# Attention backward with column tiles: dQ one group of four units later, a fourth buffer for the transposed dS, one for the turned dK and dV

## The chip, the cores and the metric

The kernel runs on one core of a Trainium2 chip. Its engines each have an instruction queue of their own: TensorE (PE, its weight loads as PEld), VectorE (DVE), ScalarE (ACT), GpSimd (POOL) and SyncE (SP), which here issues DMAs; 16 DMA engines move the data. The metric is the device time of one execution in microseconds (us), lower is better.

## The reference

A transformer block with adaptive layer norm (2048 tokens, width 512, 32 heads of 16, an MLP of width 1792 with squared ReLU), its output and its gradients with respect to all inputs but one. In bfloat16; the part that the change touches is the gradient of the attention.

```python
def _A_ref(x, wqkv, wo):                       # D = 512, H = 32, Dh = 16
    q, k, v = heads_of(x @ wqkv)
    p = softmax(einsum('bhqd,bhkd->bhqk', q, k) * Dh ** -0.5)
    o = einsum('bhqk,bhkd->bhqd', p, v)
    return merged(o) @ wo
...
h = layernorm(x) * (1 + ca) + sa
x = x + ga * _A_ref(h, A_wqkv, A_wo)
h = layernorm(x) * (1 + cb) + sb
x = x + gb * mlp(h)
...
_out, _vjp = jax.vjp(_f, A_x, A_wqkv, A_wo, B_w1, B_b1, B_w2, B_b2, c, w_mod)
return (_out, *_vjp(grad_out))
```

## The kernel before

The program runs in stages, one after the other: modulation and layer norm, q, k, v and the attention forward, the MLP forward and backward, then the attention backward (`attn_bwd`, L1075), and last the gradients of the qkv weights, of x and of the modulation (`phase6`). The change lies in `attn_bwd` alone, which runs from 1640.82 to 3639.30 us of the profiled span.

Heads are taken in pairs: a group `g` of four heads is loaded at once (`load_group`: the transposed q and dO, and k, q and dO by tokens), and `jp` takes its two pairs. For a pair, the 2048 keys are cut into four columns of 512 (`c`), and for each column 16 blocks of 128 queries (`ib`) follow. One column and one block is a unit, for both heads `a` of the pair. A unit does this:

- TensorE: the scores `st` (L1184) and dP, named `dp` (L1190), 128 x 512 for each head, into PSUM.
- ScalarE: `pu`, the exponential of the scores (L1194). VectorE: `ds` = `dp` times `pu` (L1195), in bfloat16, into a tile `dsg` that holds the four units of a group (`G = 4`).
- TensorE, one group later: dK and dV (`kv`, L1127), with `ds` and `pu` as moving operands, summed over the queries in `acckv` and, at the end of a column, copied out by VectorE as `kvT` (L1130), a tile of 128 x 2048 for a pair. When a pair is done, `turn` (L1136) transposes `kvT` on TensorE and ScalarE copies it to `dk_t` and `dv_t`.
- dQ needs `ds` transposed. After its four units a group issues one DMA transpose from SP (L1204), `dsg` to `dsT`, 32 blocks of 128 x 128. `dq` (L1149) takes `dsT` as weights, eight products a unit, and sums dQ of the whole pair in one PSUM bank, `accq`. The first `dq` of a pair clears the bank (L1145), the last copies it out (L1155), both on VectorE.

What orders TensorE is the program text: the stage is under `manual_schedule` for TensorE. On the other engines, a scheduler places the instructions by their dependences and the order of the text. Two lists carry work over: `pend` holds the units whose dK, dV is to come; `kv_group` runs four of them behind the second unit of the next group. `pendq` holds the units whose dQ is to come. A group's four entries are added behind its transpose (L1206), and each unit takes one off the front as long as more than `G` are there (L1197): so a group's dQ runs two groups later, one entry a unit, behind that unit's scores and dP.

Buffers come from pools, and a tile waits until the buffer that it takes over is no longer read: `ds` has three (L1090), `dsT` three (L1091), `kvT` two (L1092), `pu` nine. The loads for the next four heads (L1111 to L1118) and the next pair's masked keys and values (L458) are issued by POOL, in its queue, as soon as their buffers are free.

Of the kernel before, what the change touches and what calls it, by code (L numbers as in the profile page):

```python
# [33 lines left out]
class K:  # L34
# [1040 lines left out]
    def attn_bwd(self):  # L1075
# [7 lines left out]
        tc, nc = self.tc, self.nc  # L1083
        S, D, H, NQ, ST, SC = self.S, self.D, self.H, self.NQ, self.ST, self.SC
        G = 4
        W = 4 * DH
        with ExitStack() as es:
            qp = es.enter_context(tc.tile_pool(name="p5q", bufs=2))
            pup = es.enter_context(tc.tile_pool(name="p5pu", bufs=9))
            dsp = es.enter_context(tc.tile_pool(name="p5ds", bufs=3))  # L1090
            dtp = es.enter_context(tc.tile_pool(name="p5dt", bufs=3))  # L1091
            kvp = es.enter_context(tc.tile_pool(name="p5kv", bufs=2))  # L1092
            stp = es.enter_context(tc.tile_pool(name="p5st", bufs=2, space=PSUM))
            dpp = es.enter_context(tc.tile_pool(name="p5dp", bufs=2, space=PSUM))
            accp = es.enter_context(tc.tile_pool(name="p5acc", bufs=1, space=PSUM))
# [10 lines left out]
            pend, pendq = [], []  # L1106

            def load_group(g):
                T = {}
                for n, src in fm.items():  # L1110
                    t = qp.tile([P, S], BF16, name=f"{n}q")  # L1111
                    nc.gpsimd.dma_start(t[:], src[g])
                    T[n] = t
                for n, src in tm.items():
                    t = qp.tile([P, ST, W], BF16, name=f"{n}g")
                    with nc.allow_non_contiguous_dma(reason="128B runs"):
                        nc.gpsimd.dma_start(t[:], src.rearrange("(st p) d -> p st d", p=P)[:, :, g * W:(g + 1) * W])
                    T[n] = t  # L1118
                return T
# [12 lines left out]
            def turn(g, jp, kvT):  # L1132
                h0 = 4 * g + 2 * jp
                tp = dpp.tile([P, ST, P], BF16, name="dp")
                for st in range(ST):
                    nc.tensor.transpose(tp[:, st, :], kvT[:, st * P:(st + 1) * P], self.ident[:])  # L1136
                v = tp[:].rearrange("p s (t a e) -> p t s a e", t=2, a=2)
                for t, dst in enumerate((self.dk_t, self.dv_t)):
                    d = dst[:, :, h0 * DH:(h0 + 2) * DH].rearrange("p s (a d) -> p s a d", a=2)
                    nc.scalar.copy(d, v[:, t, :, :, 0:DH])  # L1140

            def dq(u):
                (T, g, jp, c, ib, i, dsT) = u
                if c == 0 and ib == 0:
                    nc.vector.memset(accq[:], 0.0)  # L1145
                for a in range(2):
                    col = (2 * jp + a) * DH
                    for sub in range(4):
                        nc.tensor.matmul(accq[:, ib, a, :], lhsT=dsT[:, (i * 2 + a) * 4 + sub, :],  # L1149
                                         rhs=T["K"][:, 4 * c + sub, col:col + DH], start=False, stop=False,  # L1150
                                         skip_group_check=True)
                if c == SC - 1 and ib == ST - 1:
                    h0 = 4 * g + 2 * jp
                    d = self.dq_t[:, :, h0 * DH:(h0 + 2) * DH].rearrange("p s (a d) -> p s a d", a=2)
                    nc.vector.tensor_scalar(d, accq[:], self.scale, None, ALU.mult)  # L1155

            def kv_group():
                for u in pend[:G]:
                    kv(u)
                (T, g, jp, c, ib, kvT, pu, ds) = pend[G - 1]  # L1160
                del pend[:G]
                return (g, jp, kvT) if c == SC - 1 and ib == ST - 1 else None
# [5 lines left out]
            with tc.manual_schedule(engines={mybir.EngineType.PE}):  # L1168
                for g in range(NQ):
                    Tn = load_group(g + 1) if g + 1 < NQ else None  # L1170
                    for jp in range(2):
                        if 2 * g + jp + 1 < 2 * NQ:
                            self.load_masked(masked, msrc, (2 * g + jp + 1) // 2, 1 - jp, eng=nc.gpsimd)
                        kvT = kvp.tile([P, S], BF16, name="kvT")
                        for c in range(SC):
                            c0 = 512 * c
                            for ib0 in range(0, ST, G):
                                dsg = dsp.tile([P, G, 2, 512], BF16, name="ds")
                                for i in range(G):
                                    ib = ib0 + i  # L1180
                                    q = slice(ib * P, (ib + 1) * P)
                                    sts = [stp.tile([P, 512], F32, name="st") for a in range(2)]
                                    for a in range(2):
                                        nc.tensor.matmul(sts[a][:], lhsT=T["QT"][:, q], rhs=masked["KT"][2 * jp + a][:, c0:c0 + 512],  # L1184
                                                         start=True, stop=True)
                                    if turnq and i == 3:
                                        turn(*turnq.pop(0))
                                    dp = dpp.tile([P, 2, 512], F32, name="dp")
                                    for a in range(2):
                                        nc.tensor.matmul(dp[:, a, :], lhsT=T["dOT"][:, q], rhs=masked["VT"][2 * jp + a][:, c0:c0 + 512],  # L1190
                                                         start=True, stop=True)
                                    pu = pup.tile([P, 2, 512], BF16, name="pu")
                                    for a in range(2):
                                        nc.scalar.activation(pu[:, a, :], sts[a][:], ACT.Exp, scale=self.scale)  # L1194
                                    nc.vector.tensor_tensor(dsg[:, i], dp[:], pu[:], ALU.mult)  # L1195
                                    pend.append((T, g, jp, c, ib, kvT, pu, dsg[:, i]))
                                    if len(pendq) > G:  # L1197
                                        dq(pendq.pop(0))
                                    if i == 1 and len(pend) >= G + 2:
                                        r = kv_group()  # L1200
                                        if r:
                                            turnq.append(r)
                                dsT = dtp.tile([P, 8 * G, P], BF16, name="dsT")
                                nc.sync.dma_start_transpose(dsT[:], dsg[:].rearrange("p i a k -> p (i a k)"))  # L1204
                                for i in range(G):
                                    pendq.append((T, g, jp, c, ib0 + i, i, dsT))  # L1206
                    T = Tn
                turn(*kv_group())
                while pendq:
                    dq(pendq.pop(0))  # L1210
# [264 lines left out]
```

## Time and profile before

| | us |
|---|---|
| median of 2 runs (lowest, highest) | 3818.99 (3810.42, 3827.56) |
| the profiled execution | 3816.07 |
| its span, first to last instruction | 3814.2 |
| attention backward in it | 1998.5 (1640.82 to 3639.30) |

The page cuts the span into 40 slices of 95.4 us. Each digit is the share in tenths for which the engine was busy in that slice; PEclk is TensorE's granted clock, DMA the mean share of the 16 DMA engines.

```profile
PE   5999988888767777878788787788787887788877
DVE  6222210000043653566567556566665776667755
ACT  3999999999832443345556555455554655556633
PEclk8999999999978988989889888899898999899988
DMA  3111100000134655467978878888778888788862
```

The attention forward fills slices 2 to 10: ScalarE is at 9, the DMA engines are nearly idle. The attention backward begins in the eighteenth slice and ends in the thirty-ninth: TensorE at 7 and 8, ScalarE and VectorE at 5 to 7, the DMA engines at 7 and 8, and a clock that is granted to 8 or 9 tenths.

### The profile page before, as it was taken

What the parts mean: (1) busy time and instruction counts of PE and PEld (TensorE: products, weight loads), DVE (VectorE), ACT (ScalarE), POOL (GpSimd) and SP (SyncE); (2) the same over time, 40 slices, a digit from 0 to 9 for tenths busy, and PEclk for the clock granted to TensorE, in tenths of its full rate; (3) what the DMA queues carried; (4) which work ended last, traced back from release to release, by engine and by line L of the source; (5) the groups of instructions that cost most, each with busy time, mean ns of one, the idle gap of its engine ahead of it and who ended that gap; (6) DMA issues with size and microseconds to landing.
All of it is one profiled execution on the core that took longest, in us unless ns stands there. A gap on an engine that the chain in (4) does not pass through costs nothing. (4 is left out here: it accounts for less than half of the span.)

```text
span 3814.2 us, 75626 instructions
## 1 busy us (share of the span) xinstructions
PE 3094.9 (81%) x31556; PEld 1460.3 (38%) x31556; DVE 1894.1 (50%) x2761; ACT 2354.2 (62%) x3577; POOL 371.1 (10%) x583
## 2 busy tenths in 40 slices
PE   5999988888767777878788787788787887788877
PEld 2555533333333434633333333333333333334333
DVE  6222210000043653566567556566665776667755
ACT  3999999999832443345556555455554655556633
POOL 3111100000010233010000100100001001000000
PEclk8999999999978988989889888899898999899988
DMA  3111100000134655467978878888778888788862
GB/s 127 49 49 50 50 20 6 12 11 5 38 138 146 209 147 188 131 138 145 154 140 149 147 132 136 146 142 155 148 139 142 152 149 156 137 138 155 158 192 71
DMA packets 1178339, 447.82 MB, mean 117 GB/s; under 512 B 1089162, under 2 KB 1145612, under 8 KB 1177996
## 3 DMA queue, kind: packets, MB, share of 16 engines
q1 hardware_dynamic: 1140188, 353.70, 47.2%
q0 software_dynamic: 29184, 79.59, 7.1%
q10 hardware_dynamic: 8624, 9.70, 0.8%
q8 instruction: 247, 4.05, 0.4%
q14 instruction: 96, 0.79, 0.1%
HBM read 106.83 MB, written 67.64 MB: 46 GB/s over the span
## 5 line engine op out<-in xcount | busy, mean ns | idle before, releaser
L1194 ACT ACTIVATE pu<-st 128x512 bf16<-128x512 f32 x2048 | 1105.6, 594 | 859.5 <-PE st L1184 857.9
L1195 DVE TENSOR_TENSOR ds<-dp,pu 128x1024 bf16<-128x1024 f32 x1024 | 1226.6, 1222 | 680.8 <-ACT pu L1194 413.8
L412 ACT ACTIVATE pu<-st 128x1024 bf16<-128x1024 f32 x1024 | 940.1, 1376 | 4.7 <-PE accbank L418 4.7
L1184 PE MATMUL st<-KTm,QTq 128*128 128x512 bf16 x2048 | 700.1, 400 | 39.8 <-DMA dOTq<-dOTq_d 7.4
L1149 PE MATMUL accq<-Kg,dsT 128*128 128x16 bf16 x8192 | 362.3, 171 | 366.8 <-DMA dsT<-ds 326.6
L1190 PE MATMUL dp<-VTm,dOTq 128*128 128x512 bf16 x2048 | 648.4, 400 | 0.3
L409 PE MATMUL st<-QTm,KTq 128*128 128x512 bf16 x2048 | 607.0, 377 | 6.5 <-ACT pu L412 1.5
L1149 PEld LDWEIGHTS <-dsT 128*128 128x128 bf16 x8192 | 351.0, 98 | 676.1 <-DMA dsT<-ds 419.9
L418 PEld LDWEIGHTS <-pu 128*128 128x128 bf16 x8192 | 291.2, 96 | 458.7 <-ACT pu L412 408.2
L418 PE MATMUL accbank<-Vaug,pu 128*128 128x17 bf16 x8192 | 353.5, 172 | 67.6 <-DVE accbank L405 7.4
L1190 PEld LDWEIGHTS <-dOTq 128*128 128x128 bf16 x2048 | 206.8, 101 | 353.6 <-issue 172.8
L1127 PE MATMUL acckv<-ds,Qg 128*16 128x512 bf16 x2048 | 321.5, 444 | 0.6 <-DVE ds L1195 0.6
L1127 PE MATMUL acckv<-pu,dOg 128*16 128x512 bf16 x2048 | 321.5, 444 | 0.0
L427 DVE RECIPROCAL rl<-accbank 128x4 f32<-128x4 f32 x128 | 23.0, 180 | 526.0 <-PE accbank L418 525.6
L458 POOL DMA_DIRECT2D KTm<-KTq_d x120 | 59.8, 503 | 1504.7 <-PE st L1184 1502.7
L1184 PEld LDWEIGHTS <-QTq 128*128 128x128 bf16 x2048 | 123.8, 97 | 147.3 <-issue 146.4
L288 DVE TENSOR_SCALAR ev_fm<-pps,bcol 128x512 bf16<-128x512 f32 x92 | 69.1, 751 | 195.0 <-PE pps L281 194.0
L409 PEld LDWEIGHTS <-KTq 128*128 128x128 bf16 x2048 | 129.7, 96 | 35.0 <-issue 20.6
L281 PE MATMUL pps<-xhat1T,wpad 128*128 128x512 bf16 x384 | 122.8, 378 | 4.9 <-DVE ev_fm L288 3.8
L1127 PEld LDWEIGHTS <-Qg 128*16 128x16 bf16 x2048 | 80.7, 94 | 90.3 <-issue 41.8
L1127 PEld LDWEIGHTS <-dOg 128*16 128x16 bf16 x2048 | 80.6, 94 | 0.0
L545 ACT ACTIVATE rT<-ups,bias 128x512 bf16<-128x512 f32 x56 | 38.5, 687 | 52.1 <-PE ups L543 52.0
(305 smaller groups left out, 2377.0 us busy)
## 6 DMA issues: line engine op xcount, KB each, us to landing
rT_d<-rT SPq DMA_DIRECT2D x4, 1792.0 KB
rT<-rT_d SPq DMA_DIRECT2D x4, 1792.0 KB
duT_d<-duT POOLq DMA_DIRECT2D x4, 1792.0 KB, 12.5
rT_f<-rT_d SPq DMA_DIRECT2D x14, 512.0 KB
duT_f<-duT_d POOLq DMA_DIRECT2D x14, 512.0 KB, 3.8
xhat_d<-xhat SPq DMA_DIRECT2D x2, 2048.0 KB
QTq_d<-ev_fm POOLq DMA_DIRECT2D x32, 128.0 KB, 2.1
QTm<-QTq_d SPq DMA_DIRECT2D x128, 32.0 KB
```

Of the source, the lines that this page charges most:

```text
L281: nc.tensor.matmul(pt[:, :sw], lhsT=wpads[t][:, kt, g, :], rhs=xhat1T[:, kt, s0:s0 + sw], start=(kt == 0), stop=(kt == DT - 1))
L288: nc.vector.tensor_scalar(ev[:, :sw], pt[:, :sw], bc, None, ALU.add)
L409: nc.tensor.matmul(stt[:, a, :qw], lhsT=KT[:, kb * P:(kb + 1) * P], rhs=QTm[a][:, q0:q0 + qw], start=True, stop=True)
L412: nc.scalar.activation(pu[:, :, :qw], stt[:, :, :qw], ACT.Exp, scale=self.scale)
L418: nc.tensor.matmul(acc[:, a, sub, :], lhsT=pu[:, a, sub * P:(sub + 1) * P], rhs=Vaug[:, kb, heads[a], :], start=False, stop=False, skip_gr ...
L458: eng.dma_start(masked[n][j][r:r + 32, c0:c0 + cw], src[g, r:r + 32, c0:c0 + cw])
L1127: nc.tensor.matmul(acckv[r:r + DH, :], lhsT=T[n][:, ib, col:col + DH], rhs=src[:, a, :], start=(ib == 0), stop=(ib == ST - 1))
L1149: nc.tensor.matmul(accq[:, ib, a, :], lhsT=dsT[:, (i * 2 + a) * 4 + sub, :], rhs=T["K"][:, 4 * c + sub, col:col + DH], start=False, stop=F ...
L1184: nc.tensor.matmul(sts[a][:], lhsT=T["QT"][:, q], rhs=masked["KT"][2 * jp + a][:, c0:c0 + 512], start=True, stop=True)
L1190: nc.tensor.matmul(dp[:, a, :], lhsT=T["dOT"][:, q], rhs=masked["VT"][2 * jp + a][:, c0:c0 + 512], start=True, stop=True)
L1194: nc.scalar.activation(pu[:, a, :], sts[a][:], ACT.Exp, scale=self.scale)
L1195: nc.vector.tensor_tensor(dsg[:, i], dp[:], pu[:], ALU.mult)
```

## The change

Three numbers change. The dQ list is let grow to eight entries before a unit takes one off, so a group's dQ runs three groups later instead of two. The pool of `dsT` gets a fourth buffer (8 KB more in each partition), the pool of `kvT` goes from two buffers to one (4 KB less).

```diff
-            dtp = es.enter_context(tc.tile_pool(name="p5dt", bufs=3))
-            kvp = es.enter_context(tc.tile_pool(name="p5kv", bufs=2))
+            dtp = es.enter_context(tc.tile_pool(name="p5dt", bufs=4))
+            kvp = es.enter_context(tc.tile_pool(name="p5kv", bufs=1))
...
-                                    if len(pendq) > G:
+                                    if len(pendq) > 2 * G:
                                         dq(pendq.pop(0))
```

Every engine has as many instructions as before; ACT, POOL and SP have them in the same order too. The first place is TensorE at the first unit of the stage's fifth group. The names of the tiles carry numbers: on SP, the first five transposes of the kernel before write `dsT_21057`, `dsT_21120`, `dsT_21216`, `dsT_21311` and `dsT_21407`, in this order; the changed kernel's write `dsT_21057`, `dsT_21120`, `dsT_21183`, `dsT_21279` and `dsT_21375`. Before, from the second score product on:

```order
L1184 MATMUL st_21315<-KTm1_20943,QTq_20973 128x512
L1190 LDWEIGHTS dOTq_20975
L1190 MATMUL dp_21318<-VTm0_20949,dOTq_20975 128x512
L1190 LDWEIGHTS dOTq_20975
L1190 MATMUL dp_21318<-VTm1_20951,dOTq_20975 128x512
L1149 LDWEIGHTS dsT_21216
L1149 MATMUL accq_20934<-Kg_20977,dsT_21216 128x16
```

The changed kernel at the same unit:

```order
L1184 MATMUL st_21283<-KTm1_20943,QTq_20973 128x512
L1190 LDWEIGHTS dOTq_20975
L1190 MATMUL dp_21286<-VTm0_20949,dOTq_20975 128x512
L1190 LDWEIGHTS dOTq_20975
L1190 MATMUL dp_21286<-VTm1_20951,dOTq_20975 128x512
L1149 LDWEIGHTS dsT_21120
L1149 MATMUL accq_20934<-Kg_20977,dsT_21120 128x16
```

The fifth group used the third group's transpose and now uses the second's; the place within the unit, behind scores and dP, is the same.

The second place is VectorE at the first change of head pair, from one copy of dK, dV to the next (`x6` stands for six equal rows). Before:

```order
L1195 TENSOR_TENSOR ds<-dp,pu 128x1024 x6
L1155 TENSOR_SCALAR dq_t<-accq 128x16x32
L1195 TENSOR_TENSOR ds<-dp,pu 128x1024
L1145 MEMSET accq 128x512
L1195 TENSOR_TENSOR ds<-dp,pu 128x1024 x9
L1130 TENSOR_SCALAR kvT<-acckv,kvs 128x512
```

The changed kernel at the same place:

```order
L1195 TENSOR_TENSOR ds<-dp,pu 128x1024 x10
L1155 TENSOR_SCALAR dq_t<-accq 128x16x32
L1195 TENSOR_TENSOR ds<-dp,pu 128x1024
L1145 MEMSET accq 128x512
L1195 TENSOR_TENSOR ds<-dp,pu 128x1024 x5
L1130 TENSOR_SCALAR kvT<-acckv,kvs 128x512
```

The copy of dQ out of the bank and its clearing come four units later; one `ds` still stands between the two.

## The prediction

> **What bounds the kernel now.** I read the busy times first, then the waits of TensorE, then its timeline, then a table of stretches with the granted clock. From the page and from the waits of the attention backward stage (1640.82 to 3639.30 us):
>
> ```profile
> PE 3094.9 (81%) x31556; PEld 1460.3 (38%) x31556; DVE 1894.1 (50%) x2761; ACT 2354.2 (62%) x3577; POOL 371.1 (10%) x583
> L1149 PE MATMUL accq<-Kg,dsT 128*128 128x16 bf16 x8192 | 362.3, 171 | 366.8 <-DMA dsT<-ds 326.6
> ...
> PE accq L1149 <- DMA dsT<-ds: 326.6, 138, 14.5
> PE accq L1149 <- DVE accq L1145: 39.6, 14, 2.8
> ```
>
> TensorE is the busiest engine, and in this stage nearly all that it waits for is one thing: the dQ product waits 138 times, 326.6 us in all, for the transposed dS. The next 39.6 us are the wait for the cleared accumulator at a change of head pair. A group of four units has one transpose, so 256 of them. One group without a wait, and two transposes with their first use:
>
> ```profile
> 2002.85 0.59 PE L1184 MATMUL st<-KTm,QTq 128*128 128x512 bf16 x2
> 2003.71 0.35 PE L1149 MATMUL accq<-Kg,dsT 128*128 128x16 bf16 x8
> ...
> 2017.98 5.19 SPq L1204 DMA_TRANSPOSE dsT<-ds  x1
> 2024.76 0.36 PE L1149 MATMUL accq<-Kg,dsT 128*128 128x16 bf16 x8 [0.26 <-DMA dsT<-ds]
> ...
> 2041.12 4.77 SPq L1204 DMA_TRANSPOSE dsT<-ds  x1
> 2049.01 0.39 PE L1149 MATMUL accq<-Kg,dsT 128*128 128x16 bf16 x8 [2.73 <-DMA dsT<-ds]
> ...
> 2010.22 4.82 SPq L1204 DMA_TRANSPOSE dsT<-ds  x1
> ```
>
> From issue to use at landing it takes 6.78 us (2024.76 - 2017.98) to 7.89 us (2049.01 - 2041.12). The group that starts at 2002.85 issues its transpose at 2010.22, 7.37 us after its start; its dQ comes two groups later, 0.86 us into that group (2003.71 - 2002.85). At 5.85 us a group (next table) that is wanted 2 x 5.85 + 0.86 - 7.37 = 5.2 us after the issue, and no transpose is that fast. So a wait is built into the order. What the wait costs beyond itself is in the stretches (time, busy by engine, granted clock, DMA share, GB/s):
>
> ```profile
> core 0: us, PE busy (x) PEld busy (x) DVE busy (x) ACT busy (x) POOL busy (x), PEclk, DMA share, GB/s
> 2002.85:2008.70 5.85, 5.63 (x70) 2.72 (x67) 4.71 (x5) 4.30 (x9) 0.00 (x0) 1.00 0.66 92
> 2016.47:2023.37 6.90, 6.68 (x87) 3.66 (x84) 5.73 (x6) 5.05 (x11) 1.30 (x3) 1.00 0.82 150
> 2029.49:2039.40 9.91, 7.07 (x71) 3.00 (x68) 5.93 (x7) 4.08 (x9) 0.00 (x0) 0.83 0.71 135
> 2045.25:2056.11 10.86, 8.13 (x71) 3.25 (x69) 5.75 (x6) 4.08 (x9) 1.30 (x3) 0.69 0.78 149
> 1640.82:3639.30 1998.48, 1596.70 (x16644) 729.08 (x16645) 1289.84 (x1129) 1124.66 (x2084) 146.21 (x263) 0.91 0.82 147
> ```
>
> Each of the first four is one group: undisturbed (5.85); with the turn of dK, dV (6.90); with the accumulator wait (9.91); with a 2.73 us dsT wait (10.86). In the last two the clock was 0.83 and 0.69: after a wait the products themselves run slower. The 10.86 are 5.85 + 2.73 + 2.28 of slow clock. In the undisturbed group VectorE is busy 4.71 and ScalarE 4.30 of 5.85, so TensorE's own order sets 5.85, and both drain in each group's dK, dV block; the next group does not inherit a backlog.
>
> **The change, part by part.** No instruction is added or removed.
>
> *dQ one group later.* The first use is now wanted 5.2 + 5.85 = 11.05 us after the issue, against 6.78 to 7.89 us. The common wait is covered with 3 us to spare. That removes its 326.6 us apart from the long ones, below, and the slow clock behind them. To size the clock: 256 x 5.85 = 1498 us, 16 turns x (6.90 - 5.85) = 17, and the end:
>
> ```profile
> 3628.82 0.91 PEld L1149 LDWEIGHTS <-dsT 128*128 128x128 bf16 x32
> 3638.17 1.02 PE L1149 MATMUL accq<-Kg,dsT 128*128 128x16 bf16 x32 [4.69 <-DMA dsT<-ds]
> ```
>
> From the last group's end (about 3625.6) to 3639.3 are 14 us, where the last transpose is awaited. Base 1498 + 17 + 14 = 1529. The stage has 1998.5 = 1529 + 322 (326.6 less the 4.69 at the end) + 39.6 + a rest of 108 us, which I take as the slow clock.
>
> *What stays.* The accumulator wait moves by a group with the dQ that it stands before:
>
> ```profile
> 2030.90 0.68 DVE L1155 TENSOR_SCALAR dq_t<-accq 128x512 bf16<-128x512 f32 x1
> 2031.50 1.21 DVE L1195 TENSOR_TENSOR ds<-dp,pu 128x1024 bf16<-128x1024 f32 x1
> 2032.82 0.48 DVE L1145 MEMSET accq<- 128x512 f32 x1
> 2033.35 0.34 PE L1149 MATMUL accq<-Kg,dsT 128*128 128x16 bf16 x8 [2.84 <-DVE accq L1145]
> ```
>
> VectorE's order is the same there (copy out, one ds, clear), so it costs 14 x (9.91 - 5.85) = 57 us, slow clock included. Here the Trainium skill, "TensorE: Matmul & The Clock Gate", section "HAM oscillation — how this bites in real kernels", says to avoid TensorE gaps above about 3.4 us. The row has a gap of 2.84 us with the clock at 0.83, so the trace is stricter; by the rule these waits would cost 40 us and the stage 17 us less.
>
> *The long waits*, where loads for the next four heads fill the DMA engines:
>
> ```profile
> 1902.91 0.39 PE L1149 MATMUL accq<-Kg,dsT 128*128 128x16 bf16 x8 [11.70 <-DMA dsT<-ds]
> 2149.79 0.38 PE L1149 MATMUL accq<-Kg,dsT 128*128 128x16 bf16 x8 [9.72 <-DMA dsT<-ds]
> 2420.41 0.38 PE L1149 MATMUL accq<-Kg,dsT 128*128 128x16 bf16 x8 [9.03 <-DMA dsT<-ds]
> 2926.76 0.39 PE L1149 MATMUL accq<-Kg,dsT 128*128 128x16 bf16 x8 [14.48 <-DMA dsT<-ds]
> ```
>
> A lag of one more group takes 5.85 from each: 44.9 - 23.4 = 22 us stay, with 4 x 2.28 = 9 us of slow clock. Between 0 (the loads fall elsewhere) and 45 (nothing is covered) I take 22, since the same loads still start with the same group. VectorE's rewrite of a ds buffer, three groups on, also waits for that transpose, but about a microsecond after dQ would, so it adds nothing.
>
> *Fourth dsT buffer.* Three groups are now in flight instead of two; the transpose takes the buffer that the dQ of four groups before left a group ago, as it did with three. Cost 0; the cover is that whole group, 5.85 us. *Single kvT.* The turn reads it in a pair's first group, VectorE overwrites it in the fifth: four groups, 23 us, cover the reuse. Cost 0. *POOL's queue.* The Kg load waits for the last dQ of its buffer, so it and the loads behind it start 5.85 us later; they are wanted 16 groups (94 us) on. Cost 0. *Ends.* The third group has no dQ, the end has four units more, some 1 us by the 0.91 us row of 32 loads, within the 4.69 us wait. Cost 0.
>
> Sum: 1529 + 57 + 22 + 9 = 1617 us, 381 less than 1998.5. The profiled execution took 3816.07 us (3 below the median of 3818.99): 3816 - 381 = 3435.
>
> **The rivals.** *Transfers bound.* At a DMA share of 0.82 over 7.81 us a group (1998.5 / 256), a full share would be 6.4 us: 256 x 6.4 + 14 + 31 = 1683, so 3501, the accumulator waits being absorbed. For it: the share. Against it: what the queue moves when one transpose is under way, and when two are:
>
> ```profile
> 2007.50:2009.00 1.50, 1.39 (x15) 0.67 (x13) 1.17 (x2) 1.37 (x3) 0.00 (x0) 1.00 1.29 296
> 2012.50:2015.50 3.00, 3.00 (x40) 1.36 (x38) 1.22 (x1) 1.96 (x4) 0.00 (x0) 1.00 1.11 217
> ```
>
> The stage needs 147 x 7.81 / 5.85 = 196 GB/s; one alone gets 217, two together 296, and shares go over 1. An issue of 4.8 to 5.2 us also fits into 5.85. The Trainium skill, "Perfetto Trace Analysis", section "Identifying the Most-Contended Engine", likewise calls DMA occupancy misleading; the trace agrees, with a share of 1.29.
>
> *Transposes in series.* If none overlapped the next, a group would take 6.78: 1736 + 14 + 31 = 1781, so 3599. The 296 GB/s speak against it.
>
> *No change.* The tile is there, but something else ends last, such as ds buffers or the accumulator: for this each group would have to stay near 7.81, and the 5.85 group shows no such wait.
>
> *Slower.* Three transposes and a load crowd the queue and each issue stretches. It decides when a group passes 7.81 us. Near the loads an issue was seen at
>
> ```profile
> 1892.34 11.81 SPq L1204 DMA_TRANSPOSE dsT<-ds  x1
> ```
>
> and halfway between 4.8 and 11.8 is 8.3: 256 x 8.3 = 2125, so 3943. Only the few issues at a load are like that.
>
> **How the numbers follow.** Forecast 0.70 (3400 to 3480); transfers bound 0.14 (to 3545); series 0.09; no change 0.04; slower 0.03. From 3395 (no long waits, accumulator waits without slow clock) to 3545 lie the first two and a little, about 8 in 10. A measurement tells 2% (76 us) from no change. Faster by over 2%: 0.93; within: 0.04; slower: 0.03.
>
> **What would show it.** Right: the dQ waits for dsT fall to some 25 us in a handful of places, the stage's clock rises from 0.91 to about 0.98, its length to about 1617, GB/s to above 175, and the accumulator waits stay near 40 us. Wrong: groups at 6.4 or more with a DMA share near 1 and issues over 5.85 us; or the wait moves to VectorE's ds.

## The result, and the profile after

The changed kernel takes 3469.3 us (median of 2 runs, 3466.88 to 3471.72) against 3818.99 us. The ratio is 0.908, 95% interval 0.899 to 0.918: faster by some 350 us. The forecast was 3435 us, with a range of 3395 to 3545.

From the page of the changed kernel: busy times, three of the 40-slice lines (a slice is 86.6 us here), and two groups of instructions, of which the second answers to the one shown of before.

```profile
PE 2998.7 (87%) x31556; PEld 1452.4 (42%) x31556; DVE 1876.3 (54%) x2761; ACT 2350.4 (68%) x3577; POOL 369.9 (11%) x583
...
PE   5999998888885968498998989989899998999887
...
PEclk8999999999997989699999999999999999999998
DMA  3111110000004365654999999999999999999952
...
L1195 DVE TENSOR_TENSOR ds<-dp,pu 128x1024 bf16<-128x1024 f32 x1024 | 1211.0, 1220 | 366.4 <-ACT pu L1194 269.2
...
L1149 PE MATMUL accq<-Kg,dsT 128*128 128x16 bf16 x8192 | 356.3, 170 | 92.4 <-DMA dsT<-ds 50.0
```

TensorE's idle time before the dQ products fell from 366.8 to 92.4 us, and its busy time fell too, by 96 us, with the same 31556 products: they run at a higher clock. In the second half of the span the clock's digits are 9 where they were 8 and 9, and the DMA engines stand at 9 in nearly every slice of the stage.

The waits of TensorE in the stage:

```profile
PE accq L1149 <- DMA dsT<-ds: 50.0, 7, 9.8
PE accq L1149 <- DVE accq L1145: 42.4, 15, 3.0
```

The first line was 326.6 us in 138 places. The seven that are left are one at the stage's end (5.6 us) and six beside the loads for the next four heads. Stretches of the changed kernel (one undisturbed group, one with a turn, one with the accumulator wait, one with a wait beside the loads, and the stage):

```profile
core 0: us, PE busy (x) PEld busy (x) DVE busy (x) ACT busy (x) POOL busy (x), PEclk, DMA share, GB/s
1889.80:1895.66 5.86, 5.64 (x66) 2.73 (x65) 4.71 (x5) 4.30 (x9) 0.00 (x0) 1.00 0.94 178
1946.56:1953.46 6.90, 6.68 (x87) 3.66 (x84) 5.72 (x6) 5.05 (x11) 1.29 (x3) 1.00 1.12 195
1965.17:1975.31 10.14, 7.19 (x71) 3.05 (x68) 5.79 (x7) 4.33 (x9) 0.67 (x2) 0.83 0.78 158
1849.00:1866.14 17.14, 7.25 (x70) 2.99 (x67) 4.80 (x5) 4.32 (x9) 0.00 (x0) 0.70 1.14 144
1643.49:3289.20 1645.71, 1500.17 (x16644) 719.95 (x16645) 1270.91 (x1129) 1120.90 (x2084) 145.94 (x263) 0.97 1.02 178
```

The stage took 1998.48 us and takes 1645.71. The group of 5.86 us, at full clock, is now the rule: of the 255 groups 216 take 5.86 us, and the rest are the turns, the accumulator waits, the six long ones and the stage's first three groups, which have no dQ.

### The profile page after: what moved, and what is told of

Read it like the earlier page. It is cut to its first block, busy times and chain, and to the rows that moved or that the text cites. A ratio compares the mean times of both kernels' runs of the same rounds, so it can differ in the third digit from the quotient of the medians.

```text
span 3465.0 us, 75624 instructions
## 1 busy us (share of the span) xinstructions
PE 2998.7 (87%) x31556; PEld 1452.4 (42%) x31556; DVE 1876.3 (54%) x2761; ACT 2350.4 (68%) x3577; POOL 369.9 (11%) x583
## 5 line engine op out<-in xcount | busy, mean ns | idle before, releaser
L1195 DVE TENSOR_TENSOR ds<-dp,pu 128x1024 bf16<-128x1024 f32 x1024 | 1211.0, 1220 | 366.4 <-ACT pu L1194 269.2
L1190 PE MATMUL dp<-VTm,dOTq 128*128 128x512 bf16 x2048 | 617.2, 383 | 0.1
L1149 PE MATMUL accq<-Kg,dsT 128*128 128x16 bf16 x8192 | 356.3, 170 | 92.4 <-DMA dsT<-ds 50.0
L1190 PEld LDWEIGHTS <-dOTq 128*128 128x128 bf16 x2048 | 199.7, 98 | 377.5 <-issue 199.0
L1127 PE MATMUL acckv<-ds,Qg 128*16 128x512 bf16 x2048 | 280.3, 398 | 0.6 <-DVE ds L1195 0.6
L1127 PE MATMUL acckv<-pu,dOg 128*16 128x512 bf16 x2048 | 280.3, 398 | 0.0
```

Of the source, the lines that this page charges most:

```text
L1127: nc.tensor.matmul(acckv[r:r + DH, :], lhsT=T[n][:, ib, col:col + DH], rhs=src[:, a, :], start=(ib == 0), stop=(ib == ST - 1))
```

## The experiments

Two theories to begin with. Theory L: only the later dQ counts, and its gain has two parts, the waits and the slow clock behind them. Theory B: the buffers did it. Then the shape of the clock's price, what limits the transposes, and what holds the rest back.

**The pool sizes alone.** The list limit stays at G.

```diff
-            dtp = es.enter_context(tc.tile_pool(name="p5dt", bufs=3))
-            kvp = es.enter_context(tc.tile_pool(name="p5kv", bufs=2))
+            dtp = es.enter_context(tc.tile_pool(name="p5dt", bufs=4))
+            kvp = es.enter_context(tc.tile_pool(name="p5kv", bufs=1))
```

> The two pool sizes alone (four dsT, one kvT), dQ two groups later as before. Theory L (the gain is the longer lag alone): no change, 3819 us within 1%, the dQ waits for dsT stay near 327 us in 138 places. Rival B (the transpose was held up by its buffer, and the fourth one frees it): most of the gain, about 3470 us.

3819.2 us; ratio to the kernel before 0.998, interval 0.996 to 1.001. The waits:

```profile
PE accq L1149 <- DMA dsT<-ds: 332.9, 135, 12.7
```

The buffers by themselves do nothing. Theory B falls, and the single `kvT` costs nothing either.

**The later dQ alone**, with three `dsT` and two `kvT`.

```diff
-                                    if len(pendq) > G:
+                                    if len(pendq) > 2 * G:
```

> The lag of three groups alone, with three dsT and two kvT as before. Theory L: all of the gain, 3469 us within 20, dsT waits near 50 us, since the dQ that frees the third buffer ends about 1.5 us before the transpose that takes it is issued (a group's dQ is done 5.85 us after the group's start, the transpose comes at 7.37 us). Rival B (the fourth buffer is needed): the transposes wait for the dQ of their own group, issue later, and the time lies clearly above, 3550 us or more.

3471.5 us, ratio 0.909 (0.906 to 0.912), the same as the whole change:

```profile
PE accq L1149 <- DMA dsT<-ds: 53.0, 7, 10.3
```

The fourth buffer isn't needed: in this run's trace the dQ that frees the third ends at least 1.2 us before the transpose that takes it is issued. So the whole gain comes from one number.

**Half a group and a quarter of a group later.** The same line with `G + 2` and with `G + 1`, pools as before.

> dQ two and a half groups later (list limit G + 2), pools as before. By theory L the first use is wanted 5.2 + 3.4 = 8.6 us after the issue (the third unit of a group starts 3.4 us after the first), which covers landings of 6.8 to 7.9 us: no common wait, 3469 us plus some 15 for longer waits at the loads, less up to 40 if the dK, dV block between the pair's last dQ and the next pair's first one hides the clearing of the accumulator: 3445 to 3485 us. Rival (more than latency is at work, the DMA engines are full at 6.4 us a group): 3500 us or more.

3454.63 us in its one run, inside the expected 3445 to 3485, and below the changed kernel. The waits of this kernel:

```profile
PE accq L1149 <- DMA dsT<-ds: 87.2, 34, 12.1
...
PE accq L1149 <- DVE accq L1145: 10.6, 15, 0.9
```

It waits longer for `dsT` than the changed kernel (87 against 50 us) and is not slower, since the accumulator waits fell from 42.4 to 10.6 us and with them the slow clock (behind the stage's first three groups, 12 groups have a mean clock under 0.99, against 20): the dK, dV block now lies between a pair's last dQ and the next pair's first, and copy and clearing hide in it.

> dQ two groups and one unit later (list limit G + 1), pools as before. The first use is wanted 5.2 + 1.1 = 6.3 us after the issue, so waits of 0.5 to 1.6 us stay, in about every second group: some 110 to 150 us in all. Theory C (the clock falls only behind waits of about 2 us and more): the clock stays near 0.97 and the time is 3580 to 3630 us. Rival D (slow clock comes with any wait, in proportion, a third of it): clock below 0.95, 3640 us or more.

3672.74 us in its one run, outside the range of theory C and inside that of rival D. The waits, and the stage as a whole:

```profile
PE accq L1149 <- DMA dsT<-ds: 202.6, 112, 13.7
```

```profile
1644.12:3495.72 1851.60, 1555.24 (x16644) 717.76 (x16645) 1277.15 (x1128) 1121.32 (x2084) 145.58 (x263) 0.95 0.89 158
```

The waits were larger than I had worked out (203 against 110 to 150 us), and the clock, 0.95, is at the border of the two. So I set every group's wait for `dsT` beside its granted clock, for the kernel before and this one together (255 groups each; slow means that the mean clock over the group is under 0.99):

| wait for dsT in the group, us | groups | of them slow |
|---|---|---|
| 0.15 to 1 | 51 | 0 |
| 1 to 1.5 | 43 | 2 |
| 1.5 to 2 | 49 | 9 |
| 2 to 2.5 | 37 | 16 |
| 2.5 to 3 | 23 | 20 |
| 3 to 4 | 36 | 35 |
| over 4 | 8 | 8 |

The price is a step, but a blurred one between 1.5 and 3 us, and 47 of this kernel's waits lay inside it. Neither theory as written holds: a wait under 1.5 us is nearly free of it, one over 2.5 us nearly never.

The clock's own record in these two traces shows why the step is blurred. Inside the stage the clock is granted in full or to one half, and each stretch of half clock lasts 3.41 us or a whole multiple of it and begins on a fixed grid of 3.41 us. I cut the stage along this grid. Of the periods at full clock, all 102 in which TensorE was busy for less than 45% were followed by half clock, and 1 of 817 in which it was busy for 55% or more; between the two it was 15 of 45. Full clock came back behind all 117 slow periods that were busy for 85% or more, and behind 1 of 46 others. So a wait of about 1.7 us can be enough if it lies in one period, and one of 2.8 us can get by if a border of the grid cuts it in two: of the 14 accumulator waits of the kernel before, each of 2.8 us, 2 were free, and these two the grid cuts into 1.3 and 1.5 and into 1.8 and 1.0 us.

The Trainium skill, "TensorE: Matmul & The Clock Gate", section "Part 1: The HAM clock gate (the "warmup" mystery)", tells of a free-running activity window of about 3.4 us. The traces agree with the window, by a grid of 3.41 us on which waits of one size come out both ways. They put the step lower than a whole idle window: about half of one is enough here.

**Added work in place of the wait.** This takes the clock by itself: in the kernel before, dP of each group's first unit is made three times over.

```diff
-                                    for a in range(2):
+                                    for a in (0, 1) * (3 if i == 0 else 1):
                                         nc.tensor.matmul(dp[:, a, :], lhsT=T["dOT"][:, q], rhs=masked["VT"][2 * jp + a][:, c0:c0 + 512],
```

> The kernel before with work added: in each group's first unit the two dP products are done three times over (same operands, same result), 0.86 us of TensorE work a group at full clock, just ahead of the dQ that waits for dsT. Theory C (the clock falls behind idle stretches of TensorE of 2 us and more): the filler stands in for the waits, which shrink to under 1.5 us and no longer slow the clock, so the stage loses most of the 80 to 100 us of slow clock: 3725 to 3765 us, faster with 1024 more products, at a clock above 0.95. Rival D (the slow clock has another cause, or it comes with load): no gain, 3810 us or more, clock near 0.92.

3762.8 us, ratio to the kernel before 0.983 (0.981 to 0.985): a little faster, with 1024 more products. Waits and stage:

```profile
PE accq L1149 <- DMA dsT<-ds: 161.2, 113, 15.6
PE accq L1149 <- DVE accq L1145: 29.6, 15, 2.0
```

```profile
1641.05:3571.24 1930.19, 1693.21 (x17397) 811.25 (x17669) 1292.50 (x1128) 1125.28 (x2084) 145.40 (x263) 0.97 0.84 152
```

The clock rose from 0.91 to 0.97 and the stage lost 68 us. The added work is some 190 us: an undisturbed group takes 6.45 us here against 5.86, and a group with a wait at full clock, its wait taken off, 0.86 us more than before. 165 us of the waits for `dsT` (326.6 to 161.2) and 10 of the accumulator's went: 15 us more, had the clock stayed. It is 68 less, so the slow clock gave back about 83 us; behind the stage's first three groups, 22 groups were slow where 73 had been. The waits didn't all shrink to under 1.5 us as theory C had it: 40 groups have a longer one. That idleness and not load lowers the clock here, and that this is a cost beside the wait, is thereby shown.

**A quarter more transposing.** The lag of three groups with three `dsT`, one `kvT`, and an added transpose.

```diff
                                 nc.sync.dma_start_transpose(dsT[:], dsg[:].rearrange("p i a k -> p (i a k)"))
+                                ext = dtp.tile([P, 8, P], BF16, name="ext", bufs=2)
+                                nc.sync.dma_start_transpose(ext[:], dsg[:, 0].rearrange("p a k -> p (a k)"))
```

> The lag of three groups with three dsT, one kvT, and a second transpose a group that moves the first unit's ds once more into a tile that nobody reads: a quarter more transposing, so that the cost of the transposes themselves is seen. Theory I (the issue on SP, 4.8 to 5.6 us a transpose, is the next limit): 1.25 x 5.2 = 6.5 us a group, over TensorE's 5.86, so the stage takes some 160 us more and the time is 3590 to 3660 us. Rival (the DMA engines and the issue have room for a quarter more): 3465 to 3490 us.

3665.32 us in its one run, just over the expected range, against 3471.5 for the later dQ alone (which has two `kvT`). The waits, the issues (shortest, median and longest time in ns), and the stage but for its last groups:

```profile
PE accq L1149 <- DMA dsT<-ds: 226.2, 112, 16.6
```

```profile
L1204 SPq DMA_TRANSPOSE dsT<-ds x256: 4784/5392/14731, 1657.2 to 3476.7; - x128
...
L1206 SPq DMA_TRANSPOSE ext<-ds x256: 1248/1267/8307, 1652.6 to 3474.9; - x128
```

```profile
1648.28:3482.00 1833.72, 1524.25 (x16592) 711.91 (x16593) 1282.73 (x1122) 1121.96 (x2081) 145.59 (x262) 0.95 1.14 196
```

The two issues take 5.39 + 1.27 = 6.66 us a group, more than TensorE's 5.86, and the waits are back. SP's queue is full here: from the first transpose to the last, the issues take 97% of the time, against 84% in the changed kernel, and 502 of 511 follow right behind the one before. So the changed kernel stands close below the next limit. What sets the length of an issue isn't shown, SP itself or the DMA engines behind it: both carry a quarter more, and the rate of 196 GB/s is under the 296 seen in short stretches but 18 over the changed kernel's 178.

**One more group of lag**, four in all (list limit `3 * G`), with the changed kernel's pools.

> As the changed kernel, but dQ four groups later (list limit 3 G). Six waits for dsT of 5 to 10 us are left in the changed kernel, at the loads for the next four heads, 44 us with 11 us of slow clock. Theory Q (dQ alone waits there): another 5.85 us of lag takes most of them, 3425 to 3440 us. Theory S (VectorE waits for the same transpose, since it rewrites a ds buffer three groups on; the profile shows a 9.4 us wait of VectorE beside TensorE's 9.8): the waits move from dQ to ds and TensorE waits no less, 3455 to 3475 us.

3456.14 us in its one run, as theory S has it. The wait of TensorE that came in place of the six, and that of VectorE:

```profile
PE dp L1190 <- DVE ds L1195: 37.1, 6, 8.8
```

```profile
DVE ds L1195 <- DMA dsT<-ds: 44.8, 6, 10.1
```

There are still six, for the same transposes, but by way of VectorE, which may not rewrite a `ds` buffer before it is transposed. By this, more lag alone helps the long waits little; a kernel with another `ds` buffer wasn't run.

**Three and a half groups.** The changed kernel with `2 * G + 2`.

> As the changed kernel, but dQ three and a half groups later (list limit 2 G + 2). The pair's last dQ then stands before a dK, dV block and the next pair's first dQ behind it, so clearing the accumulator hides there: 15 waits of 2.8 us with 1.3 us of slow clock each fall to some 0.7 us without it, as with two and a half groups, minus 50 us: 3410 to 3425 us by theory S (the long waits stay with VectorE's ds), 3390 to 3405 us by theory Q (they shrink by 3.4 us each as well). Neither holds if it is over 3450 us.

3411.91 us, ratio to the kernel before 0.892 (0.890 to 0.894), in theory S's range:

```profile
PE dp L1190 <- DVE ds L1195: 34.6, 7, 7.4
PE accq L1149 <- DVE accq L1145: 11.3, 15, 0.9
```

The accumulator waits fell to 0.6 to 0.9 us each, a size at which the table has no slow group; the six long ones stay, by way of VectorE (the seventh in that line is one of 0.3 us).

**The loads in SP's queue.** The changed kernel, with the loads for the next four heads on another queue and written one a column, not all at the start of the four heads (the three loads by tokens, not shown, change like the last line).

```diff
-                    Tn = load_group(g + 1) if g + 1 < NQ else None
+                    Tn = {} if g + 1 < NQ else None
...
+            spread = {(0, 1): "K", (0, 2): "QT", (0, 3): "dOT", (1, 1): "Q", (1, 2): "dO"}
...
+                            if Tn is not None and (jp, c) in spread:
+                                load_one(Tn, g + 1, spread[jp, c])
...
-                    nc.gpsimd.dma_start(t[:], src[g])
+                    (nc.sync if g else nc.gpsimd).dma_start(t[:], fm[n][g])
```

> As the changed kernel, but the loads for the next four heads are issued from SP, in its queue between the transposes (the first two together, the others one a group), not from POOL all at once. Theory V (the long waits come from the loads' packets running beside a transpose): a transpose then waits at most for 1 MB, some 4 us, which the 4 us of spare lag cover; the six long waits and their slow clock go, minus 40 to 55 us: 3415 to 3430 us. Rival (the volume of the loads delays the transposes whatever the queue): no change, 3460 to 3480 us, or slower.

3419.64 us, ratio 0.894 (0.891 to 0.897). The stage's waits for `dsT` are gone but for 3.7 us at its end:

```profile
PE accq L1154 <- DMA dsT<-ds: 3.7, 1, 3.7
```

So the six long ones came from how the loads were issued, and not from their volume. The transposes at the six loads landed 9.8 to 11.4 us after their issue, against 17.5 to 22.0 us in the changed kernel. The edit changes two things, the queue and the spacing: POOL issued the first four loads within about 6 us, SP has transposes between them. Which of the two does it isn't shown. How the loads stand in SP's queue is shown with the next kernel.

**Both together.**

> Both together: loads for the next four heads from SP's queue and dQ three and a half groups later, with the changed kernel's pools. If the six long waits and the accumulator's clearing are separate costs, the gains add: 3469 - 50 - 57 = 3362, so 3350 to 3380 us, with no wait over 1 us left inside the stage but for its start and end. Rival (both shorten the same stretches, or the half group more of lag meets the SP queue's loads): 3395 us or more.

3364.69 us, ratio to the kernel before 0.880 (0.878 to 0.881), below the changed kernel's interval. SP's queue where one set of loads begins, the accumulator waits, and the stage:

```profile
1838.59 0.38 SPq L1111 DMA_DIRECT2D dOTq<-dOTq_d  x1
1839.06 7.36 SPq L1211 DMA_TRANSPOSE dsT<-ds  x1
1846.52 0.52 SPq L1115 DMA_DIRECT2D Qg<-qtm_d  x1
1847.14 6.50 SPq L1211 DMA_TRANSPOSE dsT<-ds  x1
```

```profile
PE accq L1154 <- DVE accq L1150: 15.8, 15, 1.8
```

```profile
1647.04:3188.86 1541.82, 1453.46 (x16374) 713.95 (x16645) 1268.85 (x1128) 1120.90 (x2084) 111.74 (x227) 1.00 1.07 189
```

The gains add, and the clock is 1.00 over the whole stage. The accumulator's waits reach 1.8 us where I expected under 1, and one for `ds` is 1.5 us. The stage's 1541.8 us are within 13 of the 1529 that the prediction took as its base.

## Why the prediction was right, and where it was off

*Mechanism.* Right: a first use wanted 5.2 us after an issue that lands after 6.8 to 7.9 us must wait, one wanted after 11.05 us needn't. With the lag alone all of the gain is there, with the buffers alone none. The landing events of the traces bear it out: in the kernel before half of the transposes had landed 7.0 us after their issue and none sooner than 6.6, in the changed kernel half after 7.3 us and 9 in 10 within 9.0. The signs that the prediction named came, two of them weaker: 50 us of waits where some 25 were expected, and a stage of 1646 us for 1617; the clock is 0.97 (0.98 expected), the rate 178 GB/s (over 175), the accumulator's waits 42 us (40).

*The pace of 5.85 us.* Right: 5.86 us, 216 times. The base comes out at 256 x 5.86 + 17 + 14.6 = 1532 us against 1529.

*The slow clock, 108 us.* Its existence and its cause are shown by the added products (0.91 to 0.97, 68 us less). The size of 108 us was a remainder. It can be measured group by group: what the groups with a wait take beyond 5.86 us, the wait and 1.04 for a turn comes to 106 us in the kernel before and to 29 in the changed one. The stage's gain agrees: 1998.5 - 1645.7 = 353 us, of which 326.6 - 50.0 = 277 are waits; the accumulator waits are nearly unchanged, so some 76 us are clock. The 29 that stay, behind the accumulator and the long waits, are what the sum had (17 + 9).

*Accumulator waits, 57 us.* 15 groups take 60.9 us more than 5.86 each: right in kind, 4 us short, since 15 come and not 14.

*The long waits, 22 + 9 us.* This is the term that was mis-sized: 44.3 us of waits and 10.7 of slow clock. "A lag of one more group takes 5.85 from each" supposed the same landings, and counted only the four waits over 9 us. Six came. The four make 28.0 us in place of the 21.5 worked out, though their landings are nearly the same on the mean (19.2 us after the issue, 19.0 before): at one of them the kernel before, late by a wait just before, had wanted its transpose only after 11.7 us, so the longer lag gained 0.5 us there. The other two add 16.3. The first of the six, in the changed kernel, by issue and use:

```profile
1837.76 8.26 SPq L1204 DMA_TRANSPOSE dsT<-ds  x1
...
1859.80 0.36 PE L1149 MATMUL accq<-Kg,dsT 128*128 128x16 bf16 x7 [9.78 <-DMA dsT<-ds]
```

That is 22.0 us from issue to use, where it had been 18.2, and 9.78 instead of the 11.70 - 5.85 = 5.85 that I took. At the new, even pace the load of `Qg` (L1117) was issued 2.3 to 3.4 us after a transpose in six places of six. At the old pace it came 6.0 to 7.6 us after one in three of the six; two of these transposes landed after only 9.4 and 11.8 us, the third after 20.8. That the offset makes the difference is thus argued and not shown. The 24 us by which the two terms were short (55 against 31) are most of the 34 us by which the forecast was low; the rest is 7 us in base and accumulator waits and some 4 us outside the stage.

*Fourth dsT buffer, single kvT, POOL's queue, ends: cost 0.* Right, but for 1 us at the stage's end; the run with the lag alone shows that the fourth buffer isn't needed, and the run with the pools alone that the single `kvT` costs nothing. In the changed kernel TensorE has no wait for a load within the stage but for the 7.1 us at its start, which was there before (7.4).

*VectorE's rewrite of ds.* "About a microsecond after dQ would" was right and close: in the changed kernel VectorE waits up to 9.4 us beside TensorE's 9.8, and with more lag it is what ends last: one more group of lag took off only 13 us (3456.14 against 3469.3).

*The rivals.* Transfers bound: the share came to 1.02 with no common wait, so it was no limit, as the 196 against 217 and 296 GB/s had said. But the margin is thin: a quarter more transposing brings the waits back. Transposes in series (6.78 us a group), no change and slower fall with the 216 groups of 5.86 us.

## What to carry to other kernels

Work the lag out from two times: when the result lands after its issue, and when its first use is wanted after the same issue. A software pipeline (work that uses what an earlier round made) whose lag is short by 2 us or more can pay for it twice, once in the wait and once in TensorE's clock. A lag in whole groups can be refined by units, where half a group also decides what else hides. After such a step look at the rare waits: here they belonged to other transfers, and moving these into the queue of the waited-for transfer, spaced out, did more for them than further lag.

## What the runs showed of the hardware that I had not expected

- TensorE's clock falls behind idle stretches as short as 1.5 to 3 us: of the groups with a wait of 2 to 2.5 us 16 of 37 were slow, with one of 2.5 to 3 us 20 of 23. It is decided on a grid of 3.41 us: a period busy for less than 45% was followed by half clock 102 times of 102, one busy for 55% or more once in 817.
- Adding 1024 products of 128 x 512 made the kernel before faster: 3762.8 us, against 3826.6 for the kernel before in runs on the same chip.
- The 1.8 MB of loads for four heads, issued from POOL, four of five within about 6 us, stretched a transpose to between 17.5 and 22.0 us from issue to landing; issued from SP between the transposes, they left it at 9.8 to 11.4 us.
- The DMA share can be over 1 for a whole stage (1.02, and 1.07 in the last experiment) without a wait for the transposes.
